# Token order for v by SBUF-to-SBUF DMAs in place of 0/1 matmuls, with a new order of work

## Chip, cores and metric

The kernel runs on one core of one Trainium2 chip. The metric is the time of one execution in microseconds on the device. Engines are called PE (TensorE), DVE (VectorE), ACT (ScalarE), POOL (GpSimd) and SP (SyncE).

## The reference

Two stages, one after the other: a linear-attention recurrence over 768 tokens (4 batches, 8 heads of 48), and a mixing stage over tokens and channels (width 384).

```python
# r, k, v: (4, 8, 768, 48) float32; w, u: (8, 48)
for t in range(S):
    kt, vt, rt = k[:, :, t], v[:, :, t], r[:, :, t]
    cur = einsum('bhd,bhe->bhde', u[None] * kt, vt)
    y[:, :, t] = einsum('bhd,bhde->bhe', rt, state + cur)
    state = w[None, :, :, None] * state + einsum('bhd,bhe->bhde', kt, vt)
x = y.transpose(0, 2, 1, 3).reshape(4, 768, 384)

theta = x @ w_theta
z_r, z_i = x * cos(theta), x * sin(theta)
un = x + einsum('ts,bsd->btd', w_tok_r, z_r) + einsum('ts,bsd->btd', w_tok_i, z_i)
out = un + maximum(un @ w_ch, 0)
```

## The kernel before

The recurrence is cut into chunks of 128 tokens; two neighbouring chunks make a double chunk. There are 12 double chunks, g = 0 to 11, three for each batch. For each one `front` does this:

- SP loads k, r and v into slots of a ring `ld` of nine tiles (lines 505 and 511). A "paired" load puts two neighbouring tokens (2p, 2p+1) on partition p, in one DMA with runs of 384 B. An unpaired load takes one DMA for each chunk, with runs of 192 B. r is always paired; k and v are paired for the double chunks in `TWO` (g = 0 to 3), unpaired for the others.
- `Kw` and `Rw` (line 675) are k and r times tables of powers of w (`kpow`, `kpow2`, `rpow`). PE turns them (line 565), and ACT or DVE evacuates the result as `KT` and `RT` (lines 576 and 574), in token order.
- `scores` (line 714) multiplies KT with RT; `mAT` (line 720) masks them. `PD` (line 727), `diag` (736) and `dg` (741) give the bonus factor of u; `yd` (744) is that factor times v.
- `outer` and `outer2` (lines 759 and 773) give the sums for the state from Kw and v; `outer2` takes the paired v, called `v2`, as it is. `Sb`, `T` and `N` (lines 790 to 816) carry the state on.
- `outputs` (lines 833 and 842) multiplies RT with the state and mAT with v. `x` (line 850) adds yd.
- x is turned (`xT`, by PE or by a transposing DMA, line 585), `theta` (line 865) multiplies it with w_theta, ACT makes cosine and sine (`trig`, lines 870 and 873), and `z` (line 876) is x times both.

`mixing` then takes, for each batch, 2 x 6 products of 128x384 for each of the six token tiles (`mix`, line 896), adds x (`un`, held in `uu_all`, line 903), turns the sum, multiplies it with w_ch (`chan`, line 919), makes the output (`fin_all`, line 923) and stores it (line 929). The token weights w_tok_r and w_tok_i, w_theta and w_ch come in by casting DMAs that POOL issues (line 524); they wait for a small copy `gate` (line 699) that waits for the eighth load. PE turns the token weights into `WrT` and `WiT`.

yd and outputs need v with one token on each partition, in token order: the tile `vb`. For an unpaired load that is one cast (lines 614 and 616). For a paired load it takes three steps: a cast into `v2` (line 628 on ACT or 630 on POOL); `put` (line 639), for each of the two chunks two matmuls with `place`, a 0/1 matrix that brings the even and the odd tokens to their rows; and `put out` (line 647 on ACT or 649 on DVE), which copies the PSUM bank into `vb`:

```python
nc.tensor.matmul(bank(tv)[:, :HD], place[:, c, j, :], v2[:, :, j, :],
                 start=(j == 0), stop=(j == 1))
```

The order of the work is planned when the kernel is built. Every step is a task of the class `Plan`, with an engine, an estimated duration, what it reads and writes, and the PSUM banks that it takes (eight in all). `Plan.order` goes through time and starts on each free engine the ready task with the lowest number in the list `RANK`; this fixes the order of instructions on each engine, and on the chip each engine keeps it. Some tasks name a second engine that could do them (`alt`); those whose index stands in `MOVED` go there: casts and evacuations from ACT to DVE, Kw and PD from DVE to POOL, Rw and yd from POOL to DVE. DVE and POOL tasks marked `port` are kept apart in time, by the plan and by an added dependency. Transfers count in the plan by `xfer`, with a fixed `LANDING` of 2000 ns behind them.

The task `warm` is still planned twelve times on PE, but issues no matmul; `stuff` is the tile that it would read.

Of the kernel before, what the change touches and what calls it, by code (L numbers as in the profile page):

```python
# [34 lines left out]
class Plan:  # L35
# [50 lines left out]
    def order(self):  # L86
# [23 lines left out]
        while times or dma_next < math.inf:  # L110
# [26 lines left out]
            for e in engines:  # L137
# [23 lines left out]
                if t.xfer:  # L161
                    q = int(e == POOL)
                    queues[q].append(t)
                    if len(queues[q]) == 1:
                        todo[q] = t.xfer + ns
                else:
                    t.end = done + LAT[e]
                    for b in t.uses:
                        left[b] -= 1
                        freed[b] = max(freed.get(b, 0.0), t.end)  # L170
                        if left[b] == 0:
                            banks.append((freed[b], self.bank_of[b]))
                            heapq.heappush(times, freed[b])
                    release(t.users, t.end)
# [10 lines left out]
TWO = (0, 1, 2, 3)  # L185
W_BY_DMA = ()
WARM = 12
# [4 lines left out]
    0, 447, 446, 449, 445, 469, 470, 471, 472, 473, 474, 475, 476, 477, 478, 479, 480, 448, 450,  # L192
    451, 452, 455, 458, 463, 453, 456, 454, 457, 468, 421, 481, 482, 459, 460, 461, 462, 464,
    465, 466, 467, 399, 424, 397, 489, 574, 176, 573, 97, 485, 528, 387, 69, 195, 62, 183, 42,
    444, 490, 502, 147, 190, 144, 202, 406, 64, 571, 231, 120, 572, 28, 104, 570, 232, 27, 569,
    29, 283, 79, 130, 68, 78, 378, 382, 377, 213, 540, 210, 218, 320, 246, 217, 247, 219, 393,
    348, 204, 346, 145, 391, 230, 188, 345, 194, 390, 172, 74, 174, 73, 386, 222, 84, 221, 292,
    389, 187, 128, 131, 186, 118, 132, 321, 119, 409, 381, 584, 70, 129, 63, 215, 142, 115, 244,
    408, 224, 412, 545, 243, 544, 415, 298, 319, 288, 77, 30, 289, 146, 189, 122, 121, 200, 169,
    168, 143, 233, 416, 124, 182, 136, 137, 384, 420, 248, 170, 113, 223, 192, 237, 81, 71, 240,  # L200
    66, 75, 197, 379, 201, 410, 135, 161, 411, 245, 167, 111, 242, 112, 114, 383, 211, 216, 388,
    141, 125, 236, 46, 72, 173, 83, 673, 33, 35, 228, 32, 34, 148, 430, 521, 429, 380, 250, 542,
    251, 543, 432, 431, 523, 520, 423, 277, 414, 433, 403, 442, 404, 105, 139, 214, 434, 385,
    220, 418, 238, 193, 191, 239, 47, 48, 392, 171, 41, 209, 249, 541, 117, 76, 229, 149, 196,
    347, 102, 635, 52, 440, 365, 51, 61, 106, 80, 342, 274, 45, 367, 65, 253, 278, 279, 363, 59,
    108, 207, 375, 67, 185, 366, 178, 177, 184, 439, 640, 56, 55, 644, 138, 682, 268, 486, 353,
    267, 270, 103, 57, 364, 107, 208, 359, 441, 258, 109, 54, 637, 134, 133, 31, 260, 285, 327,
    623, 110, 356, 165, 166, 681, 427, 357, 437, 438, 351, 436, 435, 43, 227, 634, 370, 58, 344,
    343, 633, 205, 504, 631, 164, 632, 101, 1, 369, 368, 372, 275, 374, 641, 645, 127, 513, 235,
    93, 338, 611, 2, 371, 373, 212, 82, 636, 376, 261, 53, 494, 360, 159, 349, 153, 3, 487, 405,  # L210
    394, 517, 519, 286, 505, 509, 510, 498, 497, 116, 503, 514, 515, 508, 507, 156, 322, 255,
    426, 323, 643, 179, 355, 95, 98, 354, 163, 99, 341, 639, 284, 527, 642, 175, 126, 181, 362,
    38, 44, 413, 553, 290, 291, 554, 602, 624, 606, 326, 629, 269, 94, 683, 428, 678, 151, 154,
    679, 152, 150, 324, 684, 287, 526, 680, 96, 100, 325, 276, 297, 532, 531, 425, 162, 15, 17,
    160, 14, 16, 615, 350, 262, 539, 328, 301, 529, 294, 90, 91, 293, 608, 610, 206, 334, 257,
    337, 335, 88, 559, 605, 36, 419, 705, 37, 39, 664, 25, 26, 619, 358, 299, 304, 155, 352,
    300, 361, 158, 401, 565, 603, 558, 85, 4, 333, 561, 555, 618, 560, 302, 563, 600, 535, 656,
    638, 655, 630, 5, 263, 331, 332, 609, 254, 266, 264, 533, 396, 657, 628, 707, 614, 6, 506,
    516, 496, 493, 500, 546, 501, 495, 417, 499, 492, 616, 443, 525, 407, 402, 395, 601, 157,
    234, 422, 534, 308, 296, 340, 575, 576, 339, 86, 87, 330, 552, 295, 625, 336, 590, 89, 303,  # L220
    693, 594, 597, 530, 700, 398, 400, 662, 547, 548, 583, 607, 305, 591, 329, 256, 280, 557,
    593, 595, 556, 592, 598, 626, 654, 19, 587, 701, 599, 596, 589, 18, 660, 123, 620, 512, 648,
    549, 550, 676, 537, 538, 50, 627, 703, 524, 225, 710, 588, 658, 579, 580, 659, 577, 578,
    585, 661, 40, 613, 663, 586, 672, 567, 568, 706, 49, 282, 22, 23, 281, 20, 21, 199, 699,
    653, 669, 309, 564, 709, 704, 581, 511, 317, 617, 318, 621, 7, 671, 647, 241, 566, 652, 702,
    646, 582, 484, 307, 180, 226, 604, 8, 708, 691, 689, 140, 670, 694, 686, 259, 491, 311, 265,
    312, 252, 9, 690, 687, 696, 551, 685, 697, 562, 518, 522, 651, 622, 649, 203, 10, 272, 695,
    316, 310, 698, 273, 688, 314, 488, 668, 60, 665, 92, 11, 315, 306, 677, 483, 313, 692, 650,
    612, 667, 271, 666, 536, 674, 24, 675, 198, 12, 13,
# [3 lines left out]
    61, 102, 105, 107, 112, 120, 140, 143, 155, 165, 173, 176, 185, 206, 222, 235, 238, 247,  # L233
    255, 267, 290, 377, 378, 390, 409, 412, 421, 441, 453, 542, 573, 593, 605, 615, 702,
# [18 lines left out]
def kernel(  # L253
# [16 lines left out]
    C = 128  # L270
# [12 lines left out]
    def bank(tok):  # L283
        return bank_t[P.bank_of[tok]]
# [4 lines left out]
    def ring(n, shape, dt, nm):  # L289
        return [sb.tile(shape, dt, name=f"{nm}{i}") for i in range(n)]  # L290
# [10 lines left out]
    stuff = sb.tile([C, 2 * C], BF16, name="stuff")  # L301
    gate = sb.tile([1, 1], F32, name="gate")
    place = sb.tile([C, 2, 2, C], BF16, name="place")
# [12 lines left out]
    v2s = ring(len(TWO), [C, H, 2, D], BF16, "v2")  # L316
# [38 lines left out]
    def setup():  # L355
# [15 lines left out]
        def stuff_fill():  # L371
            nc.vector.memset(stuff, 1.0)
            nc.vector.memset(stuff.rearrange("p (a b) -> p a b", b=2)[:, :, 1], -0.5)
        P.add(DVE, 250, stuff_fill, wr=["stuff"], prio=-102)
        for i in range(WARM):
            def warm_up(i=i):
                for _ in range(0):
                    nc.tensor.matmul(bank(("warm", i))[:, :2 * C], stuff[:, :C], stuff,
                                     start=True, stop=True)
            P.add(PE, 427, warm_up, rd=["stuff"], acq=[("warm", i)], prio=-92, name="warm")  # L380

# [51 lines left out]
        def placing():  # L433
            nc.gpsimd.memset(place, 0.0)
            nc.gpsimd.affine_select(
                out=place, in_=place, compare_op=Alu.not_equal, fill=1.0, base=0,
                channel_multiplier=-2, pattern=[[C, 2], [-1, 2], [1, C]])
        P.add(POOL, 1200, placing, wr=["place"], prio=-94)

# [3 lines left out]
        P.add(SP, 800, wu_load, wr=["wu"], prio=-90 + 0.0055, xfer=300)  # L443
# [5 lines left out]
        P.add(PE, 300, wu_flip, rd=["wu", "ident_f"], acq=["wu"], prio=-90)  # L449
# [144 lines left out]
    def front(b, base):  # L594
# [3 lines left out]
        for pr in range(NP):  # L598
# [22 lines left out]
            i2 = g % len(v2s)  # L621
            v2 = v2s[i2]
            def cast2(eng, v2=v2, iv=slots[pr][2]):
                src = Ls[iv].rearrange("p c h d -> p (c h d)").rearrange(
                    "p (h q) -> p h q", h=H)[:, :, :2 * D]
                dst = v2.rearrange("p h j d -> p h (j d)")
# [7 lines left out]
            for c in range(2):  # L634
                tv = ("V", g, c)

                def put(tv=tv, c=c, v2=v2):
                    for j in range(2):
                        nc.tensor.matmul(bank(tv)[:, :HD], place[:, c, j, :], v2[:, :, j, :],
                                         start=(j == 0), stop=(j == 1))  # L640
                P.add(PE, 340, put, rd=[("v2", i2), "place"], wr=[kv[c]], acq=[tv],
                      prio=base + 10 * pr + 1, name="put")

                def put_out(eng, tv=tv, c=c, vb=vb):
                    src = bank(tv)[:, :HD].rearrange("p (h d) -> p h d", h=H)
                    if eng is nc.scalar:
                        eng.activation(vb[:, c], src, Act.Copy)
                    else:
                        eng.tensor_copy(vb[:, c], src)
                P.add(ACT, act_ns(HD, False), lambda f=put_out: f(nc.scalar), use=[tv],  # L650
                      wr=[kv[c]], prio=base + 10 * pr + 1, name="put out",
                      alt=(DVE, dve_ns(HD), False, lambda f=put_out: f(nc.vector)))
        prev = None
        for pr in range(NP):
# [50 lines left out]
            for c in range(2):  # L705
# [11 lines left out]
                P.add(PE, 330, scores, rd=kKT + kRT, wr=[("mAT", mi, hi) for hi in range(2)], acq=tk, prio=pb + 2, mode=1,  # L717
# [272 lines left out]
```

## Time and profile before

| | |
|---|---|
| time, median of 3 runs | 143.91 us (141.71 to 144.53) |
| profiled execution, time | 140.77 us |
| profiled execution, span | 139.1 us |
| granted PE clock, mean | 0.98 |
| busy PE / DVE / ACT / POOL | 124.2 / 107.8 / 75.8 / 73.5 us |
| DMA traffic | 25.24 MB in 72637 packets, 67241 of them under 512 B |
| chain that ended last | PE 47%, DMA 16%, POOL 13%, DVE 12%, issue 6%, ACT 3% |

The span is the time between the first and the last instruction of the profiled execution; its own time is 1.67 us longer. In rows of groups the columns are the line, the engine, the operation, output and input tiles, the shapes, the count, then the busy time in us and the mean ns of one. The names are those of the tiles as the trace gives them: v2 stands as `v`, and landing places of weights stand under the tile that they borrow (`x`, `z`, `uu_all`, `fin_all`). Rows of a line give min/median/max ns and first and last start. A row of the slices has 40 digits, each the busy share of 3.5 us in tenths. In timelines the first two columns are start and duration in us; SPq is SP's sequencer, where DMAs are issued. In rows of waits the columns are the total us, the count and the longest.

### The profile page before, as it was taken

What the parts mean: (1) busy time and instruction counts of PE and PEld (TensorE: products, weight loads), DVE (VectorE), ACT (ScalarE), POOL (GpSimd) and SP (SyncE); (2) the same over time, 40 slices, a digit from 0 to 9 for tenths busy, and PEclk for the clock granted to TensorE, in tenths of its full rate; (3) what the DMA queues carried; (4) which work ended last, traced back from release to release, by engine and by line L of the source; (5) the groups of instructions that cost most, each with busy time, mean ns of one, the idle gap of its engine ahead of it and who ended that gap; (6) DMA issues with size and microseconds to landing.
All of it is one profiled execution on the core that took longest, in us unless ns stands there. A gap on an engine that the chain in (4) does not pass through costs nothing.

```text
span 139.1 us, 4098 instructions
## 1 busy us (share of the span) xinstructions
PE 124.2 (89%) x1677; PEld 84.6 (61%) x1677; DVE 107.8 (77%) x200; ACT 75.8 (55%) x142; POOL 73.5 (53%) x60
## 2 busy tenths in 40 slices
PE   2389876999999999999999989999799999999980
PEld 2168655876777666677657657675455665656640
DVE  6189989797897799989799889988689665526381
ACT  7969985899965634789413767339751305000010
POOL 6027989994055594996687899499640000000000
PEclk9999999599999999999999999999999999999996
DMA  2899999999989989999997998999862023255644
GB/s 61 230 323 321 308 222 202 195 244 210 207 174 220 194 169 226 152 209 185 158 223 133 233 255 179 223 147 232 169 232 51 7 57 66 106 167 61 170 176 163
DMA packets 72637, 25.24 MB, mean 182 GB/s; under 512 B 67241, under 2 KB 72618, under 8 KB 72618
## 3 DMA queue, kind: packets, MB, share of 16 engines
q1 hardware_dynamic: 70186, 22.03, 77.2%
q0 software_dynamic: 2432, 2.95, 12.2%
q8 instruction: 13, 0.21, 0.6%
q14 instruction: 6, 0.05, 0.2%
HBM read 20.06 MB, written 4.72 MB: 178 GB/s over the span
## 4 chain that ended last, share of the span: by engine, by line
PE 47%; DMA 16%; POOL 13%; DVE 12%; issue 6%; ACT 3%; SPq 0%; POOLq 0%; DVEq 0%; ACTq 0%
PE bank L896 23%; PE bank L919 7%; DMA fin_all<-in_moe_w_tok_r_dram 6%; PE bank L565 6%; POOL PD L727 5%; DMA ld<-in_k_dram 4%; PE bank L865 4%; POOL Rw L675 3%; DMA uu_all<-uu_all 3%; DVE mAT L720 3%; DMA ld<-in_r_dram 3%; POOL yd L744 2%; POOL Kw L675 2%; DVE fin_all L923 2%; ACT KT L576 1%
## 5 line engine op out<-in xcount | busy, mean ns | idle before, releaser
L896 PE MATMUL bank<-z,WrT 128*128 128x384 bf16 x144 | 46.8, 326 | 0.1
L896 PE MATMUL bank<-z,WiT 128*128 128x384 bf16 x144 | 46.8, 326 | 0.0
L720 DVE TENSOR_TENSOR mAT<-bank,mask 128x512 bf16<-128x512 f32 x48 | 30.9, 681 | 2.1 <-PE bank L714 2.0
L727 POOL TENSOR_TENSOR PD<-RT,KT 128x1024 bf16<-128x1024 bf16 x10 | 21.2, 2123 | 2.2 <-DVE z L876 1.1
L675 POOL TENSOR_TENSOR Kw<-ld,kpow 128x768 bf16<-128x768 f32 x7 | 12.7, 1811 | 16.7 <-DVE z L876 8.5
L870 ACT ACTIVATE trig<-bank,pi 128x384 f16<-128x384 f32 x24 | 13.7, 599 | 12.1 <-issue 4.5
L923 DVE SCALAR_TENSOR_TENSOR fin_all<-bank,uu_all 128x384 f32<-128x384 f32 x24 | 12.9, 553 | 9.1 <-PE bank L919 8.9
L896 PEld LDWEIGHTS <-WrT 128*128 128x128 bf16 x144 | 14.1, 98 | 8.4
L896 PEld LDWEIGHTS <-WiT 128*128 128x128 bf16 x144 | 14.1, 98 | 8.3 <-issue 0.2
L903 DVE TENSOR_TENSOR uu_all<-bank,x 128x384 bf16<-128x384 f32 x24 | 13.1, 552 | 6.0 <-PE bank L896 5.3
L744 POOL TENSOR_TENSOR yd<-dg,vb 128x768 bf16<-128x768 f32 x10 | 14.7, 1472 | 3.1 <-ACT dg L741 1.8
L675 POOL TENSOR_TENSOR Rw<-ld,rpow 128x768 bf16<-128x768 f32 x8 | 14.5, 1813 | 2.3 <-PE bank L565 1.4
L919 PE MATMUL bank<-Wch,uu_all 128*128 128x384 bf16 x72 | 14.3, 326 | 1.3 <-DMA uu_all<-uu_all 0.9
L576 ACT ACTIVATE KT<-bank 128x1024 bf16<-128x1024 bf16 (+1 forms) x11 | 10.8, 981 | 8.5 <-PE bank L565 7.3
L865 PE MATMUL bank<-Wth,xT 128*128 128x384 bf16 x72 | 14.5, 326 | 0.0
L576 ACT ACTIVATE RT<-bank 128x1024 bf16<-128x1024 bf16 (+1 forms) x12 | 11.8, 986 | 3.8 <-PE bank L565 3.8
L850 DVE TENSOR_TENSOR x<-bank,yd 128x384 bf16<-128x384 f32 x24 | 12.4, 548 | 1.7 <-issue 0.9
L876 DVE TENSOR_TENSOR z<-x,trig 128x1536 bf16<-128x1536 bf16 x12 | 12.1, 1009 | 0.8 <-ACT trig L873 0.8
L873 ACT ACTIVATE trig<-bank 128x384 f16<-128x384 f32 x24 | 11.9, 512 | 0.0
L565 PE MATMUL bank<-ident,Rw 128*128 128x128 bf16 x96 | 8.1, 230 | 2.5 <-DVE Rw L675 2.4
L919 PEld LDWEIGHTS <-uu_all 128*128 128x128 bf16 x72 | 6.6, 98 | 5.8 <-DMA uu_all<-uu_all 1.3
L576 ACT ACTIVATE uu_all<-bank 128x384 bf16<-128x384 bf16 x1 | 0.5, 490 | 16.7 <-PE bank L565 16.7
(105 smaller groups left out, 190.5 us busy)
## 6 DMA issues: line engine op xcount, KB each, us to landing
ld<-in_r_dram SPq DMA_DIRECT2D x12, 384.0 KB, 4.8
out_dram<-fin_all SPq DMA_DIRECT2D x11, 384.0 KB, 2.8
ld<-in_k_dram SPq DMA_DIRECT2D x16, 192.0 KB, 4.9
ld<-in_v_dram SPq DMA_DIRECT2D x16, 192.0 KB, 5.6
ld<-in_k_dram SPq DMA_DIRECT2D x4, 384.0 KB, 4.9
ld<-in_v_dram SPq DMA_DIRECT2D x4, 384.0 KB, 5.8
x<-in_moe_w_tok_i_dram POOLq DMA_DIRECT2D x1, 384.0 KB, 6.2
z<-in_moe_w_tok_r_dram POOLq DMA_DIRECT2D x1, 384.0 KB, 7.6
```

The source lines that it names most:

```text
L565: nc.tensor.matmul(bank16(tok)[:, i * C:(i + 1) * C], s, ident, is_transpose=True, start=(i == 0), stop=(i == n - 1))
L576: nc.scalar.activation(dst, src, Act.Copy)
L675: eng.tensor_mul(X[:, :, hs, :D], src[:, :, hs], pw[:, :, hs])
L720: P.add(DVE, dve_ns(HP * C), lambda hi=hi, tk=tk, mAT=mAT: nc.vector.tensor_mul(mAT[:, hi], bank(tk[hi]).rearrange("p (h t) -> p h t", h=H ...
L727: eng.tensor_mul(PD, RT, KT)
L744: eng.tensor_mul(yd.rearrange("p a h d -> p (a h) d"), wide(dg, D), vb.rearrange("p a h d -> p (a h) d"))
L865: nc.tensor.matmul(bank(th)[:, :HD], xT[:, t, dk, :], Wth[:, dk, :], start=(dk == 0), stop=(dk == ND - 1))
L870: P.add(ACT, act_ns(HD, False) + 65 + (1300 if g == 0 and t == 0 else 0), lambda th=th, t=t, trig=trig: nc.scalar.activation(trig[:, t, 0] ...
L896: nc.tensor.matmul(bank(tm)[:, :HD], (WrT, WiT)[ri][:, so, to * C:(to + 1) * C], z[:, so, ri], start=(part == 0 and i == 0), stop=(part == ...
L903: P.add(DVE, dve_ns(HD), lambda tm=tm, t=t, to=to, un=un: nc.vector.tensor_add(un[:, t], bank(tm)[:, :HD], x[:, to]), use=[tm], rd=[("x", ...
L919: nc.tensor.matmul(bank(tf)[:, :HD], uT[:, t, dk, :], Wch[:, dk, :], start=(dk == 0), stop=(dk == ND - 1))
L923: nc.vector.scalar_tensor_tensor(fin[:, t], bank(tf)[:, :HD], 0.0, un[:, t], op0=Alu.max, op1=Alu.add),
```

## The change

`TWO` takes in g = 4, so k and v of the fifth double chunk are loaded paired too. `v2` gets the layout [token pair, j, head, d], so that one token's row is contiguous, and a ring of four tiles. `put`, `put out`, `place`, `stuff` and the warm tasks go. In their place one ACT task `order` issues four DMAs on ACT's queue for each of the five double chunks, each moving 64 rows of 768 B from v2 to every second partition of vb. Some estimates of the plan change, the plan learns a negative `xfer` as a time that a result takes to land, and `RANK` and `MOVED` are new (684 tasks in place of 711, 29 moved in place of 35).

```diff
-                if t.xfer:
+                if t.xfer > 0:
...
-                    t.end = done + LAT[e]
+                    t.end = done + LAT[e] - min(t.xfer, 0.0)
...
-TWO = (0, 1, 2, 3)
+TWO = (0, 1, 2, 3, 4)
...
-    v2s = ring(len(TWO), [C, H, 2, D], BF16, "v2")
+    NV2 = 4
+    v2s = ring(NV2, [C, 2, H, D], BF16, "v2")
...
-        def stuff_fill():
-            nc.vector.memset(stuff, 1.0)
-            nc.vector.memset(stuff.rearrange("p (a b) -> p a b", b=2)[:, :, 1], -0.5)
...
-        def placing():
-            nc.gpsimd.memset(place, 0.0)
-            nc.gpsimd.affine_select(
-                out=place, in_=place, compare_op=Alu.not_equal, fill=1.0, base=0,
-                channel_multiplier=-2, pattern=[[C, 2], [-1, 2], [1, C]])
-        P.add(POOL, 1200, placing, wr=["place"], prio=-94)
...
-        P.add(SP, 800, wu_load, wr=["wu"], prio=-90 + 0.0055, xfer=300)
+        P.add(SP, 800, wu_load, wr=["wu"], prio=-90 + 0.0055, xfer=900)
...
-        P.add(PE, 300, wu_flip, rd=["wu", "ident_f"], acq=["wu"], prio=-90)
+        P.add(PE, 300, wu_flip, rd=["wu", "ident_f", ("lw", 1)], acq=["wu"], prio=-90)
...
-                dst = v2.rearrange("p h j d -> p h (j d)")
+                src = src.rearrange("p h (j d) -> p j h d", j=2)
+                dst = v2
...
-            for c in range(2):
-                tv = ("V", g, c)
-
-                def put(tv=tv, c=c, v2=v2):
-                    for j in range(2):
-                        nc.tensor.matmul(bank(tv)[:, :HD], place[:, c, j, :], v2[:, :, j, :],
-                                         start=(j == 0), stop=(j == 1))
...
-                def put_out(eng, tv=tv, c=c, vb=vb):
-                    src = bank(tv)[:, :HD].rearrange("p (h d) -> p h d", h=H)
...
+            def order_v(vb=vb, v2=v2):
+                for c in range(2):
                     for j in range(2):
+                        nc.scalar.dma_start(
+                            out=vb[j::2, c].rearrange("p h d -> p (h d)"),
+                            in_=v2[c * Dp:(c + 1) * Dp, j].rearrange("p h d -> p (h d)"))
+            P.add(ACT, 1100, order_v, rd=[("v2", i2)], wr=kv, prio=base + 10 * pr + 1,
+                  xfer=-2500, name="order")
...
-                P.add(PE, 330, scores, rd=kKT + kRT, wr=[("mAT", mi, hi) for hi in range(2)], acq=tk, prio=pb + 2, mode=1,
+                P.add(PE, 240, scores, rd=kKT + kRT, wr=[("mAT", mi, hi) for hi in range(2)], acq=tk, prio=pb + 2, mode=1,
...
-                                    Kw[:n, j, 2 * hp + hi, :], v2[:n, 2 * hp + hi, j, :],
+                                    Kw[:n, j, 2 * hp + hi, :], v2[:n, j, 2 * hp + hi, :],
...
-            ns = (210 if last else 430) if two else (110 if last else 310)
+            ns = (300 if last else 620) if two else (150 if last else 400)
```

## The prediction

> **What bounds the kernel now.** I read the page first (busy time, the slices, the chain that ended last), then the windows of 5 us, then the puts by their line, the waits, and the timelines of TensorE, ScalarE, GpSimd and SyncE up to 60 us.
>
> ```profile
> span 139.1 us, 4098 instructions
> PE 124.2 (89%) x1677; PEld 84.6 (61%) x1677; DVE 107.8 (77%) x200; ACT 75.8 (55%) x142; POOL 73.5 (53%) x60
> PE   2389876999999999999999989999799999999980
> DMA  2899999999989989999997998999862023255644
> ```
>
> TensorE (PE) is busy for 89% of the span, and in the slices it is full from about 28 us on to the end, while the DMA row is full from 5 to 103 us. The windows (columns: stretch, its length, then PE, PEld, DVE, ACT and POOL busy us, clock, DMA share, GB/s) show where TensorE still has air:
>
> ```profile
> 10.00:15.00 5.00, 5.00 (x127) 3.75 (x125) 4.83 (x8) 4.64 (x12) 4.04 (x3) 1.00 1.17 321
> 15.00:20.00 5.00, 4.03 (x84) 3.04 (x79) 4.46 (x9) 4.66 (x8) 4.65 (x6) 1.00 1.09 264
> 20.00:25.00 5.00, 3.32 (x76) 2.76 (x75) 4.76 (x11) 3.15 (x6) 4.89 (x5) 0.91 1.19 200
> 25.00:30.00 5.00, 4.86 (x85) 3.87 (x83) 4.08 (x7) 4.12 (x6) 4.98 (x6) 0.74 1.21 227
> 30.00:35.00 5.00, 4.76 (x94) 3.56 (x91) 4.09 (x9) 4.99 (x12) 2.92 (x3) 1.00 1.20 208
> 95.00:100.00 5.00, 3.83 (x64) 2.25 (x63) 3.24 (x7) 4.66 (x11) 3.99 (x4) 1.00 1.03 212
> ```
>
> From 10 to 135 us the windows leave 5.45 us of idle on TensorE: 2.65 between 15 and 25, 0.38 between 25 and 35, 2.42 after that, half of it in the last row shown. So the end is set by the sum of TensorE's work plus those holes. Up to 25 us VectorE, ScalarE and GpSimd are close to full too, each behind the loads.
>
> **The change part by part.** The reading below counts the plan's tasks in the order in which the code adds them (711 before, 684 after) and looks up the numbers of both MOVED lists.
>
> *The puts.* Four double chunks lose four 128x384 matmuls and two copies each:
>
> ```profile
> L639 PE MATMUL bank<-v,place x16: 326/326/527, 9.3 to 32.7; 128*128 128x384 bf16 x16
> L647 ACT ACTIVATE vb<-bank x7: 485/498/595, 10.2 to 36.0; 128x384 bf16<-128x384 f32 x7
> L649 DVE CAST vb<-bank x1: 549/549/549, 19.9 to 19.9; 128x384 bf16<-128x384 f32 x1
> ```
>
> In TensorE's timeline the puts hold up what follows by 1.3 us at 9.3, 0.7 at 13.7, 0.7 at 18.4, and 0.33 twice at 31.9 and 32.6: 3.4 us. The fifth double chunk now takes the outer product with 32 instead of 24 matmuls; the chain has 0.62 us for 32 of that shape and 0.49 for 24, so 0.13 comes back. Bounds: only the 0.67 us after 25 us, where TensorE hardly waits, are surely worth their length; all 3.4 are worth it if inputs also come sooner. The window from 10 to 15 is full on TensorE, so the early puts do delay transposes and scores there, but VectorE at 4.83 of 5 sits right behind. I take 0.67 and two thirds of the other 2.7, since TensorE is the fuller of the two there, less 0.13: **-2.3 us**.
>
> *The copies and the issues on ScalarE.* Gone: 7 x 0.513 = 3.6 us. Added: 5 x 4 = 20 DMA issues, which the trace of before doesn't show on this engine. The nearest rows are SyncE's:
>
> ```profile
> 0.81 0.35 SPq L356 DMA_DIRECT2D z<-in_w_dram  x1
> 1.23 0.43 SPq L505 DMA_DIRECT2D ld<-in_k_dram  x1
> 10.56 1.12 SPq L505 DMA_DIRECT2D ld<-in_v_dram  x1
> 18.96 6.44 SPq L505 DMA_DIRECT2D ld<-in_r_dram  x1
> ```
>
> An issue into an empty queue takes 0.35 to 0.43 us; behind other loads it takes 1.12, and with the queue full up to 6.44. ScalarE's own queue holds nothing but these moves, so I take 0.43: 8.6 us; low end 7.0 (0.35), high end 22.4 (1.12). The other edits take from ScalarE: three casts of v less (-2.5), two paired casts more (+1.7), two token-weight evacuations, one of KT and two of Sb to VectorE (-1.6, -1.0, -0.7), one of xT back (+0.8): -3.3. Together 8.6 - 3.6 - 3.3 = +1.7 us. Its cover is ScalarE's idle time between 5 and 45 us, 7.2 us by the windows, but 10 to 20 and 30 to 35 hold only 0.7 of it. What queues behind an issue is the evacuation of KT and RT, then the Sin of the first theta: I book **+0.3 us**; 0 if all is covered.
>
> *The DMA traffic.* One double chunk's move is 128 x 2 x 384 x 2 B = 0.197 MB in 256 rows of 768 B. At the 321 GB/s of 10 to 15 us that is 0.61 us; by the SyncE queue's mean packet (77.2% of 16 x 139.1 us over 70186 packets, 24.5 ns for 314 B) it is 256 x 60 ns / 16 = 0.96 us. Five make 3.1 to 4.8 us on engines that are full. Back comes the finer loading of the fifth double chunk: k and v in 2 loads with 2048 packets in place of 4 with 4096, which by 24.5 ns is 3.1 us and by the spacing of the issues (2.29 us for a pair of halves, 1.15 for a paired load) 2.3. Net 0 to +2.5 us of queue time between 10 and 40; most of it lies under TensorE's other work, so I book **+0.3**, with +2.5 as the end.
>
> The Trainium skill, in "DMA: Bandwidth & Descriptors", section "Issuing engines are not separate DMA queues", speaks against the move: DMAs from the scalar queue run on the same 16 engines as all others, and a second issuing engine saves only issue time. The share of 1.17 and 1.19 in the rows above agrees that there is no free engine to send them to. By that rule alone the whole +2.5 would stand in place of the +0.3, and the sum below would be -1.6.
>
> *When v is there.* Now a put and its copy end about 1.3 us after the cast. The moves end after four issues (1.7) and a landing, for which the nearest are the SBUF-to-SBUF transposes, median 3.1 us, and loads, up to 5.8: 4 to 7 us. The first user, the output product of the first double chunk, starts at 15.07 with its cast done at 9.05, so that is hidden. For the fourth the cast ends at 29.4 and its outputs run at 37.5; also hidden, by 1 us in the worse case. The outer product reads v2 itself and waits for no move. Cost **0**; where the order of work is tighter it is the 3 to 4 us by which v is later.
>
> *Tables, fills, banks.* GpSimd loses the 0/1 matrix (0.52 + 0.64), VectorE two fills (0.27 + 0.17), all before the first load lands at about 7 us, and twelve warm tasks issue no instruction. Eight uses of PSUM banks go. **0.**
>
> *The new order.* Of all tasks that can run on two engines GpSimd hands five PD products (5 x 2.12) and two Kw (2 x 1.81) to VectorE, and gets one Rw (1.81) and two yd (2 x 1.47) back; with the v2 cast (0.83) and the table that is 11.5 us less on GpSimd. VectorE gets 3.4 + 1.9 for them, 3.2 for two casts of v, 1.9 for evacuations, and loses 3.6 (yd), 1.25 (Rw), 0.55 and 0.44: **+4.5 us**, 107.8 to 112.3. Between 10 and 105 us VectorE is busy for 84 of 95 us now, so this cuts its slack from 11 to 6.5. In return GpSimd stops being late:
>
> ```profile
> PE bank L565 <- POOL Kw L675: 0.6, 1, 0.6
> PE bank L565 <- DMA x<-in_moe_w_tok_i_dram: 1.0, 1, 1.0
> PE bank L736 <- POOL PD L727: 0.8, 2, 0.5
> PE bank L736 <- DVE PD L727: 0.7, 1, 0.7
> ```
>
> These four waits are 3.1 of TensorE's 5.45 us. The cast of w_theta also gets the lowest rank among the weight casts: now GpSimd issues it third at 17.87, and theta starts at 27.84. Bounds: all 5.45 filled, or as much again opened because an order worked out from estimates fits the chip worse. I take two thirds of the four waits: **-2.1 us**.
>
> **Sum.** -2.3 + 0.3 + 0.3 - 2.1 = -3.8. On the profiled execution (span 139.1, time 140.77, so 1.67 around it) that is 137.0 us. The runs shown have a median of 143.91, 3.14 above the profiled one; the same -3.8 there gives 140.1. A measurement of this kernel tells about 2% (2.9 us) from no change, so this stands somewhat beyond it; its own range is 138.1 (the puts and the four waits whole) to 141.9 (the puts at 0.67).
>
> **The rivals.**
>
> *Swallowed.* The puts' time goes into VectorE's queue: only the 0.67 us after 25 us are kept, the new holes equal the old. For: VectorE at 4.83 and 4.76 of 5 in the early windows, and 4.5 us more for it to do. Against: GpSimd loses 11.5. Time: 143.91 - 0.67 + 0.13 + 0.3 = 143.7, with 141.1 to 146.7 within 2%.
>
> *ScalarE's queue holds ScalarE up.* An issue there takes what SyncE's take under load, 1.12 us. 20 x 1.12 - 3.6 - 3.3 = 15.5 us more on ScalarE, nearly all between 8 and 45 us, against 7.2 idle: 8.3 over. The late Sin delays the first mixing product, now at 36.5, which is TensorE's filler from there on. Of the 8.3 TensorE can fill the transposes of token weights and other double chunks' scores; with half of it lost: 143.9 + 4.2 - 0.7 = 147.4. It decides from about 0.9 us per issue (18 - 6.9 - 7.2 = 3.9 over). For: the rows of 1.12 and 6.44. Against: these wait behind their own queue's loads. Late v adds to this side with 3 us where a use is close.
>
> *The moves make the loads late.* +2.5 us of transfers all in the full stretch, TensorE then waits for weights and k: 143.9 + 2.5 - 0.7 = 145.7. For: the full DMA row. Against: the packets saved for the fifth double chunk come in the same stretch.
>
> That the change doesn't do what it says (v not moved by DMA) has no sign in the diff.
>
> **How the numbers follow.** Forecast 0.50, of which 0.07 lies in the upper end of its own range, within 2%. Swallowed 0.14, all within 2%. ScalarE's queue 0.24, all slower. Late loads 0.12: 0.04 at its price, within 2%, and 0.08 with the 3 us of late v on top (148.7), slower. Faster 0.43; same 0.07 + 0.14 + 0.04 = 0.25; slower 0.24 + 0.08 = 0.32. The range reaches from 137.5, where also the rest of the 5.45 us begins to close, to 148, past ScalarE's queue: about one in ten outside on either side.
>
> **What would show it.** Right: no rows of the puts; TensorE's busy time some 3 us less; holes between 10 and 35 us below 2.5; 20 issues on ScalarE's queue with about 0.43 us each; the first mixing product before 36 us; GpSimd near 62 us and VectorE near 112. Wrong: issues near or over 1 us with KT, RT or Sin evacuations late behind them (ScalarE's queue), outputs or yd waiting for vb's DMA (late v), VectorE waits for nothing while TensorE waits for VectorE (swallowed), later landings of k and weights at the same issue times (late loads).

## The result and the profile after

The changed kernel takes 149.27 us (median of four runs, 148.31 to 149.86), the kernel before on the same chip 142.81: a ratio of 1.057 with a 95% interval of 1.045 to 1.069. Ratios, here and below, compare only runs in the chip's faster state, so they need not be the ratio of the medians. By its ratio the change costs some 8 us (6.5 by the medians), where a gain down to 140.1 was forecast; the time lies above the range of 137.5 to 148.

The page of the changed kernel, the lines that answer to those shown of before:

```profile
span 148.1 us, 4105 instructions
PE 127.5 (86%) x1669; PEld 88.3 (60%) x1669; DVE 109.0 (74%) x207; ACT 69.4 (47%) x130; POOL 62.7 (42%) x53
PE   2469997960989998679999999999999999999990
DMA  3899989999999899999999999967451165252635
```

The span grew by 9.0 us: TensorE is busy 3.3 us longer, although 4.0 us of puts are gone, and idle 5.7 us longer. The windows (columns as before) show where:

```profile
10.00:15.00 5.00, 5.00 (x87) 4.48 (x85) 4.27 (x9) 2.89 (x7) 0.90 (x1) 1.00 1.16 325
15.00:20.00 5.00, 4.68 (x84) 3.83 (x78) 4.83 (x11) 2.31 (x5) 5.00 (x5) 1.00 1.09 297
20.00:25.00 5.00, 4.04 (x72) 3.24 (x70) 3.52 (x6) 3.83 (x6) 4.98 (x6) 1.00 0.94 145
...
30.00:35.00 5.00, 2.10 (x60) 1.87 (x58) 0.29 (x1) 2.83 (x7) 0.00 (x0) 1.00 1.15 220
35.00:40.00 5.00, 2.87 (x23) 2.54 (x24) 3.62 (x6) 0.81 (x1) 2.78 (x2) 0.66 1.16 207
...
55.00:60.00 5.00, 3.62 (x85) 2.68 (x84) 3.34 (x6) 2.27 (x4) 0.52 (x2) 1.00 1.20 209
60.00:65.00 5.00, 3.41 (x46) 1.97 (x42) 3.54 (x8) 0.92 (x2) 5.00 (x3) 1.00 0.94 184
```

There are two new holes on TensorE: 5.0 us from 32 to 37 us, and 3.0 us in all between 55 and 65. From 33.3 to 36.1 us VectorE, ScalarE and GpSimd stand still too. Before, TensorE was nearly full in both stretches. The waits (total, count, longest) name what ends them:

```profile
DVE Kw L644 <- DMA ld<-in_k_dram: 5.8, 1, 5.8
PE bank L544 <- DVE Kw L644: 5.8, 2, 5.0
POOL yd L713 <- DMA vb<-v: 4.5, 1, 4.5
ACT RT L555 <- DMA vb<-v: 3.9, 1, 3.9
```

The first hole waits for k of the fifth double chunk. The timeline of SyncE's queue, first before, then after the change, and the chain that ended last after it (all start, duration) show why this is late:

```profile
11.80 1.24 SPq L505 DMA_DIRECT2D ld<-in_k_dram  x1
13.14 1.09 SPq L505 DMA_DIRECT2D ld<-in_r_dram  x1
14.32 2.17 SPq L505 DMA_DIRECT2D ld<-in_v_dram  x1
16.58 2.29 SPq L511 DMA_DIRECT2D ld<-in_k_dram  x2
```

```profile
13.20 0.37 SPq L484 DMA_DIRECT2D ld<-in_k_dram  x1
14.61 0.37 SPq L484 DMA_DIRECT2D ld<-in_r_dram  x1
16.10 0.80 SPq L484 DMA_DIRECT2D ld<-in_v_dram  x1
21.32 0.37 SPq L484 DMA_DIRECT2D ld<-in_k_dram  x1
```

```profile
16.58 4.72 DMA vb<-v
21.30 0.02 issue
21.32 14.78 DMA ld<-in_k_dram
36.09 0.02 issue
36.11 0.97 DVE Kw L644
```

Before, the four loads were issued back to back. Now there are gaps between them, and the last one is released by a move of v. By then GpSimd has begun to issue the weight casts (from 19.19), and the load takes 14.8 us to land; issued at 16.88, ahead of the casts, it takes 5.4 us (run e5 below). The list of the built program tells what ties a load to a move (line, what is written and read, what is waited for; first a row of ScalarE, then two of SyncE):

```
L617 DMACopy vb1_105<-v21_101 64x384 [waits DMAHW3_49]
...
L484 DMACopy ld2_87<-in_v_dram 128x8x96 [waits DMAHW7_49,Activation_49]
L484 DMACopy ld3_88<-in_k_dram 128x8x96 [waits DMAHW3_49]
```

In this program the DMAs of SyncE and ScalarE share eight completion counters, DMAHW0 to DMAHW7; GpSimd's have others. The eight are dealt out in the order of the program, whichever of the two engines issues, and a DMA that takes a counter waits until the DMA before it on that counter has landed. So at most eight DMAs of both queues together are under way. Before, all eight belonged to SyncE. With the moves, the load of k (the last row) has the counter of the second move of the second double chunk. ScalarE casts the v of that move from 15.02 to 15.85 only and issues it at 16.58; it lands at 21.30, and the load is issued at 21.32.

### The profile page after: what moved, and what is told of

Read it like the earlier page. It is cut to its first block, busy times and chain, and to the rows that moved or that the text cites. A ratio compares the mean times of both kernels' runs of the same rounds, so it can differ in the third digit from the quotient of the medians.

```text
span 148.1 us, 4105 instructions
## 1 busy us (share of the span) xinstructions
PE 127.5 (86%) x1669; PEld 88.3 (60%) x1669; DVE 109.0 (74%) x207; ACT 69.4 (47%) x130; POOL 62.7 (42%) x53
## 4 chain that ended last, share of the span: by engine, by line
PE 47%; DMA 22%; POOL 10%; ACT 7%; DVE 4%; issue 4%; ACTq 2%; SPq 1%; POOLq 0%; DVEq 0%
PE bank L865 24%; DMA ld<-in_k_dram 10%; DMA vb<-v 6%; PE bank L888 6%; PE bank L544 6%; PE bank L834 6%; POOL PD L696 4%; DMA ld<-in_v_dram 3%; DMA ld<-in_r_dram 2%; POOL Rw L644 2%; POOL yd L713 2%; ACT RT L555 2%; PE bank L811 2%; ACTq L617 2%; PE bank L683 1%
## 5 line engine op out<-in xcount | busy, mean ns | idle before, releaser
L713 POOL TENSOR_TENSOR yd<-dg,vb 128x768 bf16<-128x768 f32 x12 | 18.2, 1519 | 21.8 <-issue 8.3
L872 DVE TENSOR_TENSOR uu_all<-bank,x 128x384 bf16<-128x384 f32 x24 | 13.2, 552 | 10.6 <-PE bank L865 10.2
L644 POOL TENSOR_TENSOR Rw<-ld,rpow 128x768 bf16<-128x768 f32 x9 | 16.3, 1816 | 7.3 <-DVE Kw L644 7.3
L834 PE MATMUL bank<-Wth,xT 128*128 128x384 bf16 x72 | 15.5, 349 | 0.5 <-ACT xT L555 0.5
L644 POOL TENSOR_TENSOR Kw<-ld,kpow 128x768 bf16<-128x768 f32 x5 | 9.1, 1818 | 14.6 <-DVE uw L455 12.0
L888 PE MATMUL bank<-Wch,uu_all 128*128 128x384 bf16 x72 | 14.8, 326 | 0.1
L555 ACT ACTIVATE KT<-bank 128x1024 bf16<-128x1024 bf16 (+1 forms) x10 | 9.8, 981 | 10.6 <-PE bank L544 10.2
L544 PE MATMUL bank<-ident,Kw 128*128 128x128 bf16 x96 | 9.6, 257 | 5.8 <-DVE Kw L644 5.8
L644 DVE TENSOR_TENSOR Kw<-ld,kpow 128x768 bf16<-128x768 f32 (+1 forms) x8 | 7.8, 977 | 8.3 <-DMA ld<-in_k_dram 5.8
L696 POOL TENSOR_TENSOR PD<-RT,KT 128x1024 bf16<-128x1024 bf16 x5 | 10.6, 2123 | 3.5 <-ACT RT L555 3.5
L544 PEld LDWEIGHTS <-Kw 128*128 128x128 bf16 x96 | 7.3, 114 | 6.9 <-DVE Kw L644 6.1
```

The source lines that it names most:

```text
L544: nc.tensor.matmul(bank16(tok)[:, i * C:(i + 1) * C], s, ident, is_transpose=True, start=(i == 0), stop=(i == n - 1))
L555: nc.scalar.activation(dst, src, Act.Copy)
L644: eng.tensor_mul(X[:, :, hs, :D], src[:, :, hs], pw[:, :, hs])
L696: eng.tensor_mul(PD, RT, KT)
L713: eng.tensor_mul(yd.rearrange("p a h d -> p (a h) d"), wide(dg, D), vb.rearrange("p a h d -> p (a h) d"))
L834: nc.tensor.matmul(bank(th)[:, :HD], xT[:, t, dk, :], Wth[:, dk, :], start=(dk == 0), stop=(dk == ND - 1))
```

## The experiments

**First: the plan run anew.** Four kernels changed one part and let the plan work out the order from the same ranks.

```diff
# e1: the moves out, puts and copies back    e2: before, with moves for its puts
# e3: moves, and 4 unread 128x384 matmuls    e4: the moves on GpSimd's queue
-            P.add(ACT, 1100, order_v, ...)
+            P.add(PE, 340, put, ...) ; P.add(ACT, act_ns(HD, False), put_out, ...)   # e1
+            P.add(PE, 680, dense, ...)                                               # e3
+            P.add(POOL, 3000, order_v, ...)                                          # e4
```

> The new order, estimates and the fifth paired double chunk stay; the moves of v are taken out and 0/1 matmuls with their copies put back for all five double chunks, each put at the rank of the move that it replaces. Theory A (the moves tie the two DMA queues together: each DMA on ScalarE's or SyncE's queue waits until the eighth DMA before it in program order has landed, so loads, moves and ScalarE hold each other up): the load of k of the fifth double chunk is issued before 16 us instead of 21.3, TensorE's hole of 5.0 us at 32 us goes, time 140 to 144. Rival B (the new order of work is at fault by itself): the hole at 32 us stays, time 147 to 150. Rival C (TensorE stays at half speed up to 29 us because the dense 128x384 matmuls are gone): transposes of 8 blocks take 0.62 us from 12 us on, and part of the loss, 2 to 4 us, goes even if the hole stays.

Measured 154.58 us against 141.4, ratio 1.096 [1.087, 1.104].

> The kernel before with its own ranks and four paired double chunks; only the puts and copies of these four are replaced by the moves (16 DMAs on ScalarE's queue), each at the rank of its first put. Theory A: waits of loads for moves and of moves for loads appear, at least one load is issued 3 us or more later than before, time 146 to 150. Rival B: within 1.5 us of the kernel before. Rival C: the loss comes with transposes of 314 ns up to some 25 us and without late loads; 145 to 147.

Measured 167.64, ratio 1.184 [1.171, 1.197].

> The changed kernel with four dense 128x384 matmuls per paired double chunk added on TensorE right after each move is issued, into a bank that nobody reads; moves and order stay. Theory A: the late loads and the two holes stay, within 1.5 us of the changed kernel (148 to 150.5). Rival C: transposes fall from 314 to 219 ns from some 12 us on, TensorE's busy time falls in spite of 20 more matmuls, time 144 to 147. Rival B: no difference.

Measured 159.5, ratio 1.129 [1.118, 1.139].

> The changed kernel with the 20 moves issued on GpSimd's queue instead of ScalarE's; planned there with 3.0 us for four. Theory A: SyncE's loads no longer wait for moves, ScalarE never waits with a move at its head; k of the fifth double chunk is issued before 16 us and the hole at 32 us shrinks to under 2 us; GpSimd pays some 15 us of issue time, of which 85 us idle covers most: 143 to 147. Rival (the moves cost by their transfer and landing, wherever they are issued): landings of 4.4 us or more, time 149 or above. Rival C: TensorE still at 314 ns per transpose early.

Measured 157.53, ratio 1.117 [1.109, 1.126].

None of the four tells the theories apart: all are slower than the changed kernel itself, and but for e4's (149 or above) no time that was named was met. In e1 k of the fifth double chunk is issued at 15.41, as theory A said, and the time still goes the other way. The likely reason, not shown by itself, is that one changed duration or task shifts the start of all that follow in the plan, so that a list of ranks fits only the costs for which it was found. These plans with changed tasks or costs lose 10 to 18%. From here on the order of all other instructions is held, and only what a task emits is changed.

**The moves taken out, and the moves added to the kernel before.**

```diff
# e5: changed kernel                        # e7: kernel before, in the first put of a pair
-    nc.scalar.dma_start(out=vb[j::2, c]...) +    nc.scalar.dma_start(out=unread[j::2, c]..., in_=v2[...])
+    pass    # vb filled once               # e8: kernel before: put and put out emit nothing
# e6: changed kernel
-    nc.scalar.dma_start(out=vb[j::2, c]..., in_=v2[...])
+    nc.gpsimd.dma_start(out=vb[j::2, c]..., in_=v2[...])
```

> The changed kernel with its exact order of instructions, but the 20 moves are left out; vb of the first five double chunks is filled once with a constant at the start instead, so their v is missing from two products. This is the price of the moves in this order. Theory A (shared completion counters couple the queues, loads and v come late): k of the fifth double chunk is issued by 16 us, the holes at 32 and 57 us go, 139 to 142. Rival B (the new order itself): 147 or more. Rival C (TensorE cold without the dense matmuls): transposes still at 314 ns up to 25 us or later, and 2 to 4 us of the loss stay: 143 to 146.

Measured 140.04 against 141.12, ratio 0.997 [0.992, 1.001]. Theory A holds, by time and holes: both are gone, and k of the fifth double chunk is issued at 16.88 (a little after the 16 that was expected). So the moves, with all that waits for them, account for the whole loss. Rival B falls.

> The kernel before in its exact order, with puts and copies; the cast writes v2 in the new layout, and for each of the four paired double chunks the four moves are issued on ScalarE's queue in addition, into tiles that nobody reads. So nothing waits for their data. Theory A: loads wait for moves on SyncE's queue and moves wait for loads on ScalarE's, 145 to 150. Rival D (only 16 issues of 0.61 us, 9.7 us on ScalarE): 142.5 to 145 with the loads issued when they are before. Rivals B, C and E: no difference, 140.5 to 142.5.

Measured 152.41, ratio 1.085 [1.076, 1.094], a little beyond theory A. Nobody reads these moves, and yet they cost 11 us. The timeline of ScalarE in this run shows the worst place:

```profile
32.26 11.12 ACTq L642 DMA_DIRECT2D unread<-v  x4
43.44 0.49 ACT L881 ACTIVATE trig<-bank 128x384 f16<-128x384 f32 x1 [10.79 <-DMA unread<-v]
```

Four issues stretch over 11.1 us. The second, third and fourth wait 3.6, 2.9 and 2.8 us for counters that loads hold: each is issued when a load of k, r or v has landed, at 36.30, 39.63 and 42.90. The sine behind them waits 10.8, with all that hangs on it: the first mixing product starts at 48.9 instead of 36.5.

> The changed kernel with the order of every other instruction held as it is; only the queue that issues the 20 moves is GpSimd's instead of ScalarE's. Theory A: loads don't wait for moves any more, k of the fifth double chunk is issued by 17 us; GpSimd waits for the casts of v and pays some 0.75 us per issue, which delays its weight casts: 144 to 149. Rival D (the time of the issues on ScalarE is what counts): 141 to 144, since GpSimd has 85 us to spare. Rival E (the landing of the moves counts): 149 or more with the hole at 57 us as before.

Measured 147.67, ratio 1.053 [1.043, 1.062], within theory A's numbers. The loads are back in step (k of the fifth double chunk at 15.80), with the same moves and bytes on another queue with counters of its own, so it is the sharing of counters that had held them. But GpSimd now stands 7.7 us at a move whose cast of v isn't done, and TensorE has holes again, at other places (1.9 us between 25 and 30, 1.7 each between 35 and 40 and between 50 and 55).

> The kernel before in its exact order with the 16 puts and 8 copies left out; vb of the first four double chunks is filled once with a constant, so their v is missing from two products. This is what the removed work is worth at most with the order held. By the prediction's step: 2.3 us faster, 139 to 140. Rival C (the puts bring TensorE to full speed): transposes at 314 ns up to 25 us or later, no gain or a loss, 141 to 144.

Measured 142.01, ratio 1.004 [0.997, 1.010]: the removed work, 3.4 us on TensorE and 4.1 us of copies, was worth nothing in this order. Transposes of eight blocks take 1.03 us at 12.5 us and still at 19.7, as rival C said. TensorE isn't even freed:

```profile
PE 125.7 (89%) x1661; PEld 87.0 (62%) x1661; DVE 109.1 (77%) x199; ACT 73.1 (52%) x135; POOL 77.3 (55%) x65
```

It is busy 1.5 us longer than the kernel before (124.2), without 4.0 us of puts, as its other work now takes 5.5 us longer.

**Issue time, traffic, and TensorE's speed by themselves.**

```diff
# f1: kernel before, at the places of e7's moves
+    nc.scalar.activation(unread[:, i // 2], v2[:, i % 2], Act.Copy)      # four times
# f2: the same 16 DMAs as in e7, one row each
+    nc.scalar.dma_start(out=unread[j:j + 1, c]..., in_=v2[c * Dp:c * Dp + 1, j]...)
# f3: e8, and ahead of each paired outer product, four times
+    nc.tensor.matmul(bank(ts)[:, :HD], zero[:, :C], zero, start=True, stop=True)
# f6: changed kernel, at the place of the four moves
+    nc.tensor.matmul(spare[:, :HD], place[:, c, j, :], v2[:, j], ...)
+    nc.scalar.activation(vb[:, c], spare[:, :HD]..., Act.Copy)
```

> The kernel before in its exact order, with four extra copies of 128x384 on ScalarE at each of the four places where the run with moves into unread tiles had its four DMAs; no DMA is added. This is the time on ScalarE alone. Theory A (the shared completion counters cost, by waits in both directions): 141 to 143. Rival D (ScalarE's time is what counts): more than half of the 11 us of the run with unread moves, 147 or more.

Measured 143.99 against 141.28, ratio 1.020 [1.013, 1.028], above theory A's 143. 16 copies of 0.52 us, 8.4 us on ScalarE, cost 2.7 us; so ScalarE's time there isn't hidden, but it is a quarter of the 11 us. (The new layout of v2, which e7 and f2 share, leaves the cast as it was: 0.85 us against 0.84.)

> The kernel before in its exact order with the same 16 extra DMAs on ScalarE's queue at the same places into unread tiles, but each moves one row of 768 B instead of 64. Issues and completion counters are the same, the bytes are a 64th. Theory A: about the same loss as with the whole moves, 149 to 153, again with ScalarE held at the fourth group. Rival F (the traffic of the moves delays the loads): 141 to 143.

Measured 150.72, ratio 1.073 [1.065, 1.081], within theory A's numbers; rival F falls as the main cause. But the five runs spread from 147.92 to 151.87 (the two fastest alone give 1.054), all below the 152.29 to 152.48 of the whole moves: the other bytes are worth something, 0.4 to 4.4 us. Between f1 and f2 lie 3.9 us (the fastest run of f2) to 6.7 (the medians) that are hardly ScalarE's time (16 issues of some 0.6 us, against f1's 8.4 us of copies) or traffic. The trace of f2 shows waits for counters in both directions: SyncE's load of v waits from 10.2 to 13.03 for a move, and ScalarE's last two moves wait for loads, until 36.85 and 39.47.

> The kernel before in its exact order without puts and copies (vb of the first four double chunks filled once with a constant, so their v is missing from two products), and with four dense 128x384 matmuls of zeros ahead of each of the four paired outer products, in the bank that these then write. Rival C, now a part of my theory (the puts bring TensorE to full speed, so their removal buys nothing): transposes of eight blocks take 0.62 us from 14 us on at the latest instead of 1.03, time 1 to 3 us below the run without puts, 139 to 141. If TensorE's speed early doesn't matter: within 0.7 us of the run without puts, 141.5 to 142.7, or slower by the added matmuls.

Measured 141.53, ratio 1.000 [0.996, 1.005]. The transposes are back at 0.62 us from 13.0 us on, as the puts had had them, and the time is within 0.7 us of the run without puts. So rival C is right about the pace of the transposes and missed the time. But the 16 matmuls of zeros have the shape and number of the 16 puts, so TensorE pays for its pace what the puts had cost. What a faster pace would be worth by itself no run here shows.

> The changed kernel with the order of every other instruction held; in place of each group of four moves the four puts and two copies on ScalarE are written at the same place of the order, in PSUM banks that the plan has free there. So the new order runs without any DMA of v. Theory A: the 9 us go with the moves, 139.5 to 143, k of the fifth double chunk issued by 18 us. Rival B (the new order is bad by itself): 147 or more.

Measured 143.26, ratio 1.010 [1.005, 1.014]. The median is a little above theory A's 143 and far from rival B's 147. In this run a put may write a PSUM bank whose earlier content isn't yet all read, so some products are changed; the amount of work isn't. The new order with puts is no better than the old one, and not the cause of the loss. It is 1.3 points (1.8 us) slower than the same order without puts and moves (e5): here the removed work of five double chunks is worth something, unlike in the old order.

**Which of three ways.** Open was how the changed kernel's 9 us of span divide into late v, ScalarE held, and late loads.

```diff
# g1: changed kernel: out=unread[j::2, c] in place of vb (vb filled once)
# g2: changed kernel: nc.sync.dma_start in place of nc.scalar.dma_start
# g3: e7, with the moves only for g < 3
```

> The changed kernel in its exact order with all 20 moves on ScalarE's queue, but into tiles that nobody reads; vb of the first five double chunks is filled once with a constant, so their v is missing from two products. Theory A1 (the waits for completion counters make the loss): loads and ScalarE as in the changed kernel, k of the fifth double chunk issued after 20 us, 145 to 149. Theory A2 (the late landing of v is what counts): 140 to 143.

Measured 146.66 against 141.58, ratio 1.036 [1.030, 1.043]. Theory A1: the load of k is issued at 21.07 and the first hole stays (4.2 us between 30 and 40); the one at 55 us shrinks from 3.0 us to 0.4. Against the 1.057 of the changed kernel, whose interval begins at 1.045, about 2 points (3 us) are v that lands late; the two intervals only just miss each other. From 1.036 to the 0.997 without moves are 4 points: the waits for counters, the issues and what the bytes cost.

> The changed kernel with every other instruction held in order and the 20 moves issued on SyncE's queue at the same place of the program. ScalarE is free of them; loads now stand behind moves that wait for casts of v. If ScalarE's holding makes most of the loss: 141 to 145. If late loads make it: 148 or more, with the load of k of the fifth double chunk at or after 20 us.

Measured 155.7, ratio 1.090 [1.079, 1.102], beyond both guesses, and without the late load that the second one named. k of the fifth double chunk is issued at 17.57, earlier than in the changed kernel, but the moves of the second double chunk stand behind loads until 27.95, and yd waits 23.2 us in all for moves. So freeing ScalarE this way only makes v later; it does not tell ScalarE's holding from late loads. How the 4 points divide between them stays open, though the chain above puts the 5.0 us hole down to the late load.

> The kernel before in its exact order with the unread moves on ScalarE's queue for the first three double chunks only; the fourth group, at which ScalarE stood for 11 us in the run with four groups, is left away. Theory A (a move takes a completion counter that a slow load still holds): 142 to 145, against 152.4 with the fourth group, and no wait of ScalarE for a move over 3 us. If the cost is per move, three quarters of the 11 us stay: 149 to 150.

Measured 145.32, ratio 1.015 [1.007, 1.024]: the four runs lie from 142.91 to 146.46, about the upper end of theory A's range, and ScalarE waits at no move as long as 3 us. The fourth group alone was worth some 6 to 7 of e7's 8.5 points. It stood in the stretch of the weight casts, where loads hold their counters longest; the kernel before has up to 16.4 us there from issue to landing for a load. The first three groups together cost no more than f1's 16 copies, within the intervals. So the price is not one per move.

## Why the prediction was wrong

*What is missing in the sum* is the largest part. No term has loads that wait for moves, or moves that wait for loads. The step on ScalarE's issues took it that ScalarE's queue "holds nothing but these moves", and put every wait of one queue for the other at nothing. Both engines draw on one set of counters: with the moves the kernel is at 1.057, without them, in the same order, at 0.997 (e5). TensorE's work and holes, of which the sum was made, are no guide to this: a hole opens wherever an in-order engine stands at one late load, and that needs only one wait in the wrong place.

*The puts, -2.3 us*, failed too. Measured in the old order: nothing (e8, 1.004). The step counted the puts' time as freed and left the length of all other TensorE work as it was; that work grew by 5.5 us. The first mixing product starts at 36.5 before, 36.7 without puts and 36.9 with dense matmuls in their place (f3, 1.000). The lower bound of the step, 0.67 less 0.13, was nearer there. In the new order the puts and copies of five double chunks are worth 1.8 us (f6 against e5), so the price hangs on the order.

*ScalarE's issues, +0.3 us*, was also mis-sized. An issue takes 0.61 us, not 0.43 (min/median/max in ns, start; then ScalarE's timeline and landing):

```profile
L617 ACTq DMA_DIRECT2D vb<-v x20: 468/607/641, 9.6 to 54.8; - x20
16.58 4.49 ACTq L617 DMA_DIRECT2D vb<-v  x7
21.17 1.02 ACT L555 ACTIVATE RT<-bank 128x1024 bf16<-128x1024 bf16 x1 [3.87 <-DMA vb<-v]
vb<-v ACTq DMA_DIRECT2D x20, 48.0 KB, 4.4
```

That is about 12 us in all instead of 8.6, and in f1 such time costs a third of its length. The 3.9 us for which RT waits here are issue time, seven issues back to back from 16.58 to 21.07. ScalarE's waits for counters are short in the changed kernel, 1.1 and 0.75 us at the last two moves; in e7 they come to 9.3 us. The rival of ScalarE's queue came nearest in size, with 147.4, but by luck: its issues were to take 1.12 us and to decide from 0.9 on, and they take 0.61. What it lacked, the counters, holds SyncE's loads in the changed kernel, and opens the larger hole there.

*The traffic, +0.3 us*: not contradicted, and not confirmed. f2 leaves 0.4 to 4.4 us for the bytes, and q10, the moves' queue, has 2.5% of the engines' time. The rival of late loads was right that loads come late and wrong about why: they are issued late, and the load of k, once late, runs beside the weight casts (14.8 us to land, against 5.4 ahead of them in e5). The Trainium skill's "Issuing engines are not separate DMA queues", in "DMA: Bandwidth & Descriptors", would have put the price into the transfers; f2 has the larger part of the loss almost without them.

*When v is there, 0*: the landing was foreseen (4 to 7 us after the cast; from issue to landing 3.3 to 7.0, median 4.4), but I looked at the first and the fourth double chunk. It was the fifth: its four issues begin at 51.3, the third waits for a load of r and the last for a load of v, and yd starts at 59.9, when the move has landed. This is the 2 points of g1.

*The new order, -2.1 us*: GpSimd's load came as counted, 62.7 us (62 expected); VectorE's grew by 1.2 us, to 109.0, not by 4.5 to 112. Without the moves TensorE's holes between 10 and 135 us are 3.7 us instead of 5.45, so 1.7 us were filled. But puts and order together, -4.4 us in the sum, show in the time as at most 0.8% (e5), and with puts the order is 1% slower than the old one (f6).

What was to show the steps right failed accordingly: TensorE is busier by 3.3 us, the first mixing product starts at 44.6, and the holes between 10 and 35 us come to 4.2 us. The base of the sum was high as well: 143.91, where later medians of the same kernel are 141.1 to 141.6. And the first load lands at 4.5 us, not at about 7, which changes no term.

## What to carry to other kernels

Before a DMA is put in a compute engine's stream, look in the built program for what it waits for besides its data: here the counter that an earlier DMA of SyncE or ScalarE still held. In this program small DMAs on a second queue use up the same eight places in flight as large loads; they make loads wait, and can hold the engine that issues them until a load elsewhere has landed. Count DMAs as well as bytes, and keep small ones out of stretches with slow landings. Ask also whether removed work frees its engine, or whether the rest gets slower (e8). And test one part of a planned schedule with the order of the rest held, since a new plan changes more than the part.

## What the runs showed of the hardware

TensorE's slower pace was not foreseen: the rows of the windows show a granted clock of 1.00 from 10 to 20 us before and after the change. The same kind of eight transposes in the kernel before and in the changed one (start, duration):

```profile
12.38 0.62 PE L565 MATMUL bank<-ident,Kw 128*128 128x128 bf16 x8
```

```profile
17.01 1.03 PE L544 MATMUL bank<-ident,Kw 128*128 128x128 bf16 x8
```

In the kernel before, with dense 128x384 matmuls from 9.3 us on, they run in 0.62 us from 12 us on; in the changed kernel, without them, in 1.03 us up to 21 us and 0.89 at 29, after the first theta products. Twenty transposes back to back (from 10.72) did not bring the pace up; four dense matmuls of zeros per double chunk did (f3 against e8, 12 to 20 us). The Trainium skill, in "TensorE: Matmul & The Clock Gate", section "Part 4: PE-mode transpose", says that transposes don't count as busy for the clock gate as other matmuls do; these rows agree. But two runs don't fit dense matmuls as the whole rule: in e8 eight transposes take 0.62 us at 27.8, with no dense matmul before them, and in f2 they still take 1.03 us at 13.2 and 18.5, with puts at 9.0 and 15.3. What sets the pace is not settled here.

A move of 64 rows (the changed kernel) and one of a single row (f2) take the same time to issue on ScalarE's queue, mostly 0.5 to 0.65 us, and a move takes 0.53 us on GpSimd's (e6).
